# First batch of a Fourier mixing layer: own PSUM banks for the way back, another order inside each step, and two weight pieces finished later

## The chip, the cores and the metric

The kernel runs on one core of one Trainium2 chip. The metric is device time in microseconds (us) of one execution. TensorE does the matrix products, VectorE (DVE in the profile) and ScalarE (ACT) work on the results, GpSimd (POOL) does a few element-wise sums and issues transfers, SyncE (SP) issues most transfers.

## The reference

Two layers run one after the other. The first multiplies each of 8 batches, along its 3008 positions, by a filter in the frequency domain. The second is a two-layer network with an ELU between its two products. Cut to what matters:

```python
X = np.fft.rfft(x, axis=1)                       # x: (8, 3008, 256)
Y = X * (filt_r + 1j * filt_i)[None, :, :]       # filt: (1505, 256)
y = np.fft.irfft(Y, n=3008, axis=1).astype(np.float32)
h = y.reshape(24064, 256) @ w_in                 # w_in: (256, 2048)
g = np.where(h > 0, h, np.exp(np.minimum(h, 0)) - 1)
out = g @ w_out                                  # w_out: (2048, 256)
```

`w_in` and `w_out` arrive as 64-bit floats.

## The kernel before

**The transform.** 3008 is 47 x 64, so the transform is split into a short transform over 64 points, a multiplication by a table, and a transform over 47 points. For one batch the kernel has these stages. `a_unit` (`a_first` for batch 0) does the 64-point part for six groups of columns `c`. Then eight frequency groups `g` follow. `b_unit(b, g)` does the 47-point part on the way there and multiplies by the filter: eight records of TensorE matmuls into two PSUM banks, then four VectorE products (lines 309 to 312). `bi_unit(b, g)` is the 47-point part on the way back: sixteen records of matmuls into two banks, then two ScalarE copies out of them (lines 329 and 330). `y_write` sends the result to DRAM, and `y_read` and `n_unit` fetch it in another order and finish the transform for one of six column groups `m`.

**The first batch** goes without a trip through DRAM between its 64-point and its 47-point part. `t_first(g)` turns the stored result around by eight TensorE transposes into two PSUM banks `po`, which ScalarE copies out (line 270). Its way back takes both the filtered products and their second halves straight into the matmuls (`s[0]` and `s[1]` hold two tiles each), so nothing is added by GpSimd.

**The network.** The work on the 6 column groups of the 8 batches is cut into quads, one for each quarter `q` of the 2048 hidden columns. A quad has seven products up and seven products down (a Strassen-like scheme with seven products for eight), and ups of quad i are interleaved with downs of quad i-1. `plan` is an order written out by hand: `at(quad, place, fn)` puts a unit either in the middle of a quad (place 0) or at its end (place 1), and each engine runs its instructions in the order in which the program issues them.

**The weights** come in 16 pieces `k` of 512 columns x 128 rows, four to a quarter. `w_fetch(k)` brings a piece, `w_split(k)` (2 VectorE instructions) takes mantissa and exponent bits apart, `w_float(k)` (4 ScalarE instructions: two for the mantissa, two in `w_power` for the exponent) turns them into 32-bit floats, and `w_join(k)` (3 or 4 on VectorE) multiplies the two and stores the piece. After pieces 1, 3, 5, ... the join also runs `w_sums` (4 on VectorE), which forms the combinations that the seven products need; for piece 15 it is placed by itself. The pieces share two sets of work tiles `wtmp`, one for even and one for odd `k`; piece 15 uses the even one.

**PSUM.** There are eight banks: `po0` to `po3` (for `t_first`, later for the products down) and `m0` to `m3`, which `bank()` hands out in turn, the one freed first (in program order) being the first to be given again. From the third step of the first batch on, the same two of the four go to every `bi_unit` and the other two to every `b_unit`.

**The stretch that matters here** is the loop of the first batch at line 713, run for `g` from 0 to 9. In step `g` the program issues, in this order, the transposes for `g + 2`, the way back of `g - 2`, `w_float(g + 7)`, the forward unit of `g`, `y_write(0, g - 2)`, `w_join(g + 7)` and `w_split(g + 8)`, each where it applies. After it come the pieces 12 to 14, `y_read(0, 0)`, `n_unit(0, 0)` and then the quads.

Of the kernel before, what the change touches and what calls it, by code (L numbers as in the profile page):

```python
# [11 lines left out]
FP32 = mybir.dt.float32  # L12
# [14 lines left out]
P = 128  # L27
D = 256
# [6 lines left out]
NG = K2 // 4  # L35
# [78 lines left out]
def kernel(  # L114
# [25 lines left out]
    t2p = pool("t2p", 2)  # L140
# [3 lines left out]
    t4p = pool("t4p", 2)  # L144
# [4 lines left out]
    psO = pool("psO", 1, space=PSUM)  # L149
# [3 lines left out]
    gb, gr, gi = (gs[:, i] for i in range(3))  # L153
# [14 lines left out]
    banks = [0, 1, 2, 3]  # L168

    def bank(name, shape=(P, 2, D)):  # L170
        i = banks.pop(0)
        return i, psM.tile(list(shape), FP32, tag="m%d" % i, name=name)
# [86 lines left out]

    def t_first(g):  # L260

        t = t2s[0, g] = (t4p if g in (2, 3) else t2p).tile([P, 4, D], FP32, tag="t4" if g in (2, 3) else "t2", name="t2")
        for j in range(2):
            i = 2 * (g % 2) + j
            ps = psO.tile([P, 2, 256], FP32, name="po%d" % i)
            for u in range(2):
                k = 4 * g + 2 * j + u
                for dh in range(2):
                    nc.tensor.transpose(ps[0:ROWS, u, ts(dh, P)], zt[k // 16][dh][:, ts(k % 16, ROWS)], eye)
            nc.scalar.activation(out=t[0:ROWS, 2 * j:2 * j + 2, :], in_=ps[0:ROWS], func=AXT.Copy)  # L270
# [23 lines left out]
    def tile_mm(ps, table, k, rhs, special):  # L294
        for u, w, v in ((0, 1, 1), (1, 1, 0)) if special else ((0, 2, 0),):
            for n, r in enumerate(rhs):
                nc.tensor.matmul(ps[:, u:u + w, :], table[k, v, :], r[k, u:u + w, :], start=n == 0, stop=n == len(rhs) - 1)  # L297

    def b_unit(b, g, f=None, gb=gb, pq=None):
        t = t2s.pop((b, g))  # L300
        f = fbufs[(b * NG + g) % FBUFS] if f is None else f
        (i0, re), (i1, im) = (bank(n) for n in ("psr", "psi"))
        for o, a in ((0, 0), (64, 2)):
            for ps, k in ((re, LO), (im, HI)):
                tile_mm(ps[o:o + 64], gb, k, [t[:, a:a + 2, :]], g == 0 and a == 0)
        sr, si = (sp.tile([P, 2, D], FP32, tag=n, name=n) for n in ("sr", "si"))
        p, q = pq or (qp.tile([P, 2, D], FP32, tag=n, name=n) for n in ("sp", "sq"))

        nc.vector.tensor_tensor(out=sr, in0=re, in1=f[:, 0], op=ALU.mult)
        nc.vector.tensor_tensor(out=si, in0=re, in1=f[:, 1], op=ALU.mult)  # L310
        nc.vector.scalar_tensor_tensor(out=p, in0=im, scalar=-1.0, in1=f[:, 1], op0=ALU.mult, op1=ALU.mult)  # L311
        nc.vector.tensor_tensor(out=q, in0=im, in1=f[:, 0], op=ALU.mult)
        banks.extend((i0, i1))
        if b == 0:

            ss[b, g] = [sr, p], [si, q]
            return
        nc.gpsimd.tensor_tensor(out=sr, in0=sr, in1=p, op=ALU.add)  # L318
        nc.gpsimd.tensor_tensor(out=si, in0=si, in1=q, op=ALU.add)
        ss[b, g] = [sr], [si]  # L320

    def bi_unit(b, g):
        s = ss.pop((b, g))
        t = t3s[b, g] = t3p.tile([P, 4, D], FP32, tag="t3", name="t3")
        (i0, pa), (i1, pb) = (bank(n) for n in ("pva", "pvb"))
        for o, table, sv in ((0, gr, s[0]), (64, gi, s[1])):
            for ps, k in ((pa, LO), (pb, HI)):
                tile_mm(ps[o:o + 64], table, k, sv, g == 0 and k == LO)
        nc.scalar.activation(out=t[:, 0:2, :], in_=pa, func=AXT.Copy)  # L329
        nc.scalar.activation(out=t[:, 2:4, :], in_=pb, func=AXT.Copy)  # L330
        banks.extend((i0, i1))

    def y_write(b, g, queues=(nc.sync, nc.sync)):
        if g == 0:
# [236 lines left out]
    def w_split(k):  # L571
        m, e, c = wtmp[k % 2 if k < 15 else 0]
        f, l = c[:, 0], c[:, 1]
        wts[k] = m, e, f, l
        hi = wds[k][:, :, 1]
        nc.vector.tensor_scalar(out=m, in0=hi, scalar1=0x000FFFFF, scalar2=None, op0=ALU.bitwise_and)
        nc.vector.tensor_scalar(out=e, in0=hi, scalar1=0x7FF00000, scalar2=None, op0=ALU.bitwise_and)
# [66 lines left out]
    with tc.manual_schedule():  # L644


        with tc.tile_pool(name="boot", bufs=1) as bp:
            ff = bp.tile([P, NG, 2, 2, D], FP32, name="ff")
            once = bp.tile([P, 2, P], FP32, name="once")
            eye, gf = once[:, 0], once[:, 1].rearrange("p (v q) -> p v q", v=2)  # L650
            pq = [bp.tile([P, 2, D], FP32, name="pq%d" % i) for i in range(2)]
            zt[0] += [bp.tile([P, 16 * ROWS], FP32, name="zt%d" % i) for i in range(2)]

            for z in zt[0] + zt[1]:
                nc.gpsimd.memset(z.rearrange("p (k r) -> p k r", r=ROWS)[:, :, 48:64], 0.0)
            for k in (1, 2, 3):
                w_fetch(k)
            f_arrange()
            w_fetch(0, nc.sync)
            for c in range(NXC):  # L660
                x_place_first(c)
            for c in range(3):
                x_load_first(c)
            w_fetch(4, nc.sync)
            nc.scalar.memzero(ff[:, 0:NG // 2])
            nc.vector.memset(ff[:, NG // 2:NG], 0.0)
            wtmp.append([kp.tile([P, 512], U32, tag=t, name=n) for t, n in (("k0", "wm"), ("k1", "we"))] +
                        [kp.tile([P, 2, 512], FP32, tag="c", name="wfl")])
            wtmp.append([sdp.tile([P, 2, D], FP32, tag="sd", name=n).bitcast(U32).rearrange("p a b -> p (a b)")
                         for n in ("wm", "we")] +  # L670
                        [t1p.tile([P, XC, D], FP32, tag="t1", name="wfl").rearrange("p (a b) d -> p a (b d)", a=2)])
            for i, v in enumerate((1151.0 * 2 ** 23, 255.0 * 2 ** 23)):
                nc.vector.memset(edges[:, i:i + 1], v)

            def step(k):
                w_split(k)
                w_float(k)
                if k > 0:
                    w_join(k - 1)

            for k in range(3):
                step(k)
            w_fetch(5, nc.sync)
            for c in (3, 4):
                x_load_first(c)
            a_first(0)
            w_fetch(6, nc.sync)
            x_load_first(5)
            nc.sync.dma_start(once, once_d)
            nc.sync.dma_start(gs, gs_d)  # L690
            step(3)
            for c in (1, 2):
                a_first(c)
                w_fetch(c + 6, nc.sync)
            step(4)
            a_first(3)
            w_fetch(9, nc.sync)
            step(5)
            step(6)
            for c in (4, 5):  # L700
                a_first(c)
            tn_read(0, 0)
            for g in range(NG):
                f_read(0, g, ff[:, g])
                if 3 <= g < 5:
                    w_fetch(g + 7)
            for k in (12, 13, 14):
                w_fetch(k)
            w_split(7)
            w_join(6)  # L710
            for g in range(4):
                t_first(g)
            for g in range(NG + 2):
                if 2 <= g < NG - 2:
                    t_first(g + 2)
                if g >= 2:
                    bi_unit(0, g - 2)
                if g < 5:
                    w_float(g + 7)
                if g < NG:  # L720
                    b_unit(0, g, ff[:, g], gf, pq if g % 2 else None)
                if g >= 2:
                    y_write(0, g - 2, (nc.sync, nc.scalar if g == NG + 1 else nc.sync))
                if g < 4:
                    w_join(g + 7)
                    w_split(g + 8)
                if g == 7:
                    w_join(11)
                    w_split(12)
                    w_split(13)  # L730
            w_float(12)
            y_read(0, 0, (nc.sync, nc.scalar))
            w_float(13)
            w_join(12)
            w_fetch(15)
            w_split(14)
            w_join(13)
            w_float(14)
        for c in range(2):
            x_load(1, c)  # L740
        yp = pool("yp", 2)
# [1 line left out]
        ep = pool("ep", 2)  # L743
        op = pool("op", 1)
        n_unit(0, 0)
        w_join(14)

# [4 lines left out]
            plan.setdefault((quad, place), []).append((fn, a))  # L754


        for quad, place, fn, *a in ((0, 0, w_split, 15), (1, 1, w_float, 15, 0), (2, 0, w_float, 15, 1), (2, 1, w_join, 15),
                                    (3, 0, w_sums, 15)):
            at(quad, place, fn, *a)
        for c in range(2, XBUFS):  # L760
            at(c - 2, 0, x_load, 1, c)
# [85 lines left out]
```

## Time and profile before

| what | value |
|---|---|
| median of 4 runs | 2648.89 us (2647.28 to 2650.07) |
| the profiled execution's own time | 2647.28 us |
| its span, first to last instruction | 2645.5 us |
| PE busy | 2595.6 us (98% of the span) |
| DVE, ACT, POOL busy | 1844.0, 1507.7, 236.5 us |
| mean granted TensorE clock | 0.993 |
| PE, DVE, ACT busy from 0 to 100 us | 59.85, 70.26, 64.81 us |
| start of the loop's first forward unit on PE | 48.72 us |
| start of the last two copies of the way back (lines 329, 330) | 91.52 and 92.01 us |
| start of `n_unit(0, 0)` on PE | 100.03 us |
| first product of quad 0 | 103.57 us |

In a timeline row the first number is the start in us from the first instruction, the second the time it took, then engine, line, operation, output<-inputs, shapes and count. A square bracket tells how long the engine sat idle before the row and what ended that. Rows of like instructions that follow one another are merged (x16 is sixteen of them). In the table of windows each engine has its busy time and its number of instructions, and PEclk is the share of the TensorE clock that was granted.

### The profile page before, as it was taken

The page shows a single profiled execution, that of the slowest core. Times are in us where ns is not written, and L with a number is a line of the kernel's source. Part 1 is how long each engine was busy: PE and PEld are TensorE (multiplying, and loading weights), DVE is VectorE, ACT ScalarE, POOL GpSimd, SP SyncE. Part 2 cuts the span into 40 slices and gives each one's busy share as a digit, 9 for nine tenths or more (in the row PEclk, how much of TensorE's full clock was granted, in tenths as well). Part 3 has the DMA queues.
Part 4 walks back from the last instruction along what each step waited for, and adds up shares of the span by engine and source line. Part 5 has one row for each costly group of instructions (what it writes and reads, how often), then busy time and mean ns, then how long its engine had stood idle before and what let it go on. Part 6 is the DMA issues. An engine that isn't in the chain of part 4 may idle for free.

```text
span 2645.5 us, 37334 instructions
## 1 busy us (share of the span) xinstructions
PE 2595.6 (98%) x13508; PEld 2210.5 (84%) x13508; DVE 1844.0 (70%) x3203; ACT 1507.7 (57%) x2622; POOL 236.5 (9%) x298
## 2 busy tenths in 40 slices
PE   5899999999999999999999999999999999999998
PEld 4588789887898878988789888898789887898887
DVE  6777767677676776667767676666767677666666
ACT  6665555555556555655556555565555555555554
POOL 5001100012000210002100020001200011000000
PEclk8999999999999999999999999999999999999999
DMA  9534312523133331423214341134321333110010
GB/s 284 143 96 105 85 38 56 126 75 82 39 95 89 80 78 43 103 70 100 72 31 98 86 114 48 39 90 106 98 50 41 79 81 81 38 41 19 21 29 17
DMA packets 224456, 202.85 MB, mean 77 GB/s; under 512 B 127586, under 2 KB 191090, under 8 KB 224272
## 3 DMA queue, kind: packets, MB, share of 16 engines
q1 hardware_dynamic: 211632, 166.70, 25.2%
q0 software_dynamic: 11184, 33.04, 4.8%
q8 instruction: 107, 1.75, 0.3%
q10 hardware_dynamic: 1456, 0.72, 0.1%
q14 instruction: 77, 0.63, 0.1%
HBM read 128.52 MB, written 74.97 MB: 77 GB/s over the span
## 4 chain that ended last, share of the span: by engine, by line
PE 96%; DMA 2%; ACT 0%; DVE 0%; POOL 0%; issue 0%; ACTq 0%; DVEq 0%; SPq 0%; POOLq 0%
PE po L490 43%; PE phs L408 25%; PE phd L408 12%; PE pha L408 6%; PE psn L360 3%; PE pva L297 2%; PE psr L297 2%; PE psa L209 2%; DMA fd<-in_filt_i_dram 1%; DMA ff<-fd 0%; DMA wd<-in_moe_w_out_dram 0%; DMA fd<-in_filt_r_dram 0%; PE pvb L297 0%; DMA f<-in_moe_w_out_dram 0%; PE psi L297 0%
## 5 line engine op out<-in xcount | busy, mean ns | idle before, releaser
L490 PE MATMUL po<-g,wo 128*128 128x256 f32 (+1 forms) x5376 | 1296.7, 375 | 0.0
L490 PEld LDWEIGHTS po<-g,wo 128*128 128x128 f32 x5376 | 1015.0, 190 | 129.5 <-issue 15.8
L419 ACT ACTIVATE g<-phs 128x512 f32<-128x512 f32 (+1 forms) x576 | 338.7, 588 | 844.0 <-PE phs L408 843.4
L416 DVE TENSOR_TENSOR g<-phd,g 128x512 f32<-128x512 f32 (+1 forms) x384 | 259.6, 676 | 457.5 <-ACT e L426 282.5
L426 ACT ACTIVATE e<-e 128x512 f32<-128x512 f32 (+1 forms) x768 | 477.1, 621 | 24.3
L408 PE MATMUL phs<-y,wi 128*128 128x256 f32 (+1 forms) x1536 | 395.6, 380 | 0.0
L408 PE MATMUL phs<-ys,wi 128*128 128x256 f32 (+1 forms) x1536 | 387.6, 375 | 1.2 <-ACT g L419 1.2
L430 DVE SCALAR_TENSOR_TENSOR g<-e,g 128x512 f32<-128x512 f32 (+1 forms) x576 | 387.2, 672 | 0.0
L425 ACT ACTIVATE e<-g 128x512 f32<-128x512 f32 (+1 forms) x576 | 353.0, 613 | 32.2 <-DVE g L416 27.3
L408 PEld LDWEIGHTS phs<-y,wi 128*128 128x128 f32 x1536 | 285.1, 190 | 83.2 <-ACT t L329 34.1
L408 PEld LDWEIGHTS phs<-ys,wi 128*128 128x128 f32 x1536 | 291.5, 190 | 34.9 <-ACT g L419 1.9
L430 DVE SCALAR_TENSOR_TENSOR g<-e,phs 128x512 f32<-128x512 f32 (+1 forms) x192 | 129.9, 677 | 137.3 <-ACT e L426 137.1
L408 PE MATMUL phd<-ys,wi 128*128 128x256 f32 (+1 forms) x768 | 194.1, 375 | 0.2 <-DVE g L416 0.2
L408 PE MATMUL pha<-y,wi 128*128 128x256 f32 (+1 forms) x768 | 194.1, 375 | 0.0
L425 ACT ACTIVATE e<-phs 128x512 f32<-128x512 f32 (+1 forms) x192 | 112.9, 588 | 141.7 <-PE phs L408 140.8
L408 PE MATMUL phd<-y,wi 128*128 128x256 f32 (+1 forms) x768 | 193.7, 375 | 0.0
L318 POOL TENSOR_TENSOR sr<-sr,sp 128x512 f32<-128x512 f32 x56 | 71.2, 1271 | 1246.9 <-DVE sp L311 1246.9
L408 PEld LDWEIGHTS pha<-y,wi 128*128 128x128 f32 x768 | 146.4, 191 | 16.7
L408 PEld LDWEIGHTS phd<-ys,wi 128*128 128x128 f32 x768 | 145.5, 190 | 17.6 <-DVE g L416 1.3
L408 PEld LDWEIGHTS phd<-y,wi 128*128 128x128 f32 x768 | 145.8, 190 | 16.5
L467 DVE TENSOR_TENSOR g<-g,g 128x512 f32<-128x512 f32 (+1 forms) x192 | 130.7, 681 | 6.7
L470 DVE TENSOR_TENSOR g<-g,g 128x512 f32<-128x512 f32 (+1 forms) x192 | 130.7, 681 | 6.7
(133 smaller groups left out, 2366.6 us busy)
## 6 DMA issues: line engine op xcount, KB each, us to landing
yd<-t SPq DMA_DIRECT2D x127, 192.0 KB
t<-yd SPq DMA_DIRECT2D x190, 128.0 KB
z<-t SPq DMA_DIRECT2D x84, 256.0 KB
f<-fd POOLq DMA_DIRECT2D x112, 192.0 KB, 3.6
t<-z SPq DMA_DIRECT2D x224, 96.0 KB
out_dram<-o SPq DMA_DIRECT2D x632, 32.0 KB
tn<-tn_t SPq DMA_DIRECT2D x48, 256.0 KB
xc<-in_x_dram SPq DMA_DIRECT2D x84, 128.0 KB
```

Source lines behind the costliest of these rows:

```text
L297: nc.tensor.matmul(ps[:, u:u + w, :], table[k, v, :], r[k, u:u + w, :], start=n == 0, stop=n == len(rhs) - 1)
L318: nc.gpsimd.tensor_tensor(out=sr, in0=sr, in1=p, op=ALU.add)
L360: nc.tensor.matmul(ps[:, ts(q, P)], t[:, i - 4 * m, ds(dh * P, P)], w[:, i - 4 * m, :], start=True, stop=True)
L408: nc.tensor.matmul(ps[:, a, 0:h], w_in[q][:, COMBO[n], a, :], y[n], start=start and a == 0, stop=True, skip_group_check=True)
L416: nc.vector.tensor_tensor(out=g[o], in0=i0, in1=i1, op=ALU.add)
L419: nc.scalar.activation(out=g[o], in_=i0, func=AXT.Copy)
L425: nc.scalar.activation(out=e, in_=src, func=AXT.Relu, scale=-1.0)
L426: nc.scalar.activation(out=e, in_=e, func=AXT.Exp, scale=-1.0)
L430: nc.vector.scalar_tensor_tensor(out=g[n], in0=es[n], scalar=1.0, in1=src, op0=ALU.subtract, op1=ALU.max)
L467: nc.vector.tensor_tensor(out=b12, in0=b22, in1=b12, op=ALU.subtract)
L470: nc.vector.tensor_tensor(out=g["t4"], in0=g["b21"], in1=g["t2"], op=ALU.subtract)
L490: nc.tensor.matmul(po[i][:, u, 0:h], w_out[q][:, COMBO[n], a, :], g[n][:, a, :], start=q == 0 and a == 0 and n in (1, 3, 6, 4), stop=True, ...
```

## The change

- `bi_unit` of batch 0 takes the banks `po2` and `po3` instead of two from `bank()`; `t_first` uses `po0` and `po1` alone. The four banks of `bank()` are left to the forward units.
- In each step the matmuls of the forward unit come first, then the whole way back of `g - 2` (a function handed to `b_unit` as `between`), then the four VectorE products of the forward unit.
- The transposes for `g + 4` follow in the same step, four steps ahead instead of two; groups 6 and 7 take tiles of the pool `t4p` as groups 2 and 3 do.
- `w_float(g + 7)` stands behind the transposes. `w_join(10)` moves from step 3 to step 7, `w_split(11)` from step 3 to step 2.
- Piece 14: half of its `w_float` moves to the end of quad 0, its join to the middle of quad 1. Piece 15: the split moves from the middle of quad 0 to the end of quad 1, the halves of `w_float` from the end of quad 1 and the middle of quad 2 to the middle and end of quad 2, the join from the end of quad 2 to the middle of quad 3, the sums from the middle to the end of quad 3.
- At the start, `w_fetch(4)` is issued ahead of `x_load_first(2)`.

```diff
     def t_first(g):
-        t = t2s[0, g] = (t4p if g in (2, 3) else t2p).tile([P, 4, D], FP32, tag="t4" if g in (2, 3) else "t2", name="t2")
+        pool, tag = (t4p, "t4") if g % 4 > 1 else (t2p, "t2")
+        t = t2s[0, g] = pool.tile([P, 4, D], FP32, tag=tag, name="t2")
         for j in range(2):
-            i = 2 * (g % 2) + j
-            ps = psO.tile([P, 2, 256], FP32, name="po%d" % i)
+            ps = psO.tile([P, 2, 256], FP32, tag="po%d" % j, name="po%d" % j)
...
-    def b_unit(b, g, f=None, gb=gb, pq=None):
+    def b_unit(b, g, f=None, gb=gb, pq=None, between=None):
...
                 tile_mm(ps[o:o + 64], gb, k, [t[:, a:a + 2, :]], g == 0 and a == 0)
+        if between:
+            between()
...
     def bi_unit(b, g):
...
-        (i0, pa), (i1, pb) = (bank(n) for n in ("pva", "pvb"))
+        if b == 0:
+            pa, pb = (psO.tile([P, 2, 256], FP32, tag="po%d" % i, name="po%d" % i) for i in (2, 3))
+        else:
+            (i0, pa), (i1, pb) = (bank(n) for n in ("pva", "pvb"))
...
-        banks.extend((i0, i1))
+        if b > 0:
+            banks.extend((i0, i1))
...
-            for c in range(3):
+            for c in range(2):
                 x_load_first(c)
             w_fetch(4, nc.sync)
+            x_load_first(2)
...
             for g in range(NG + 2):
-                if 2 <= g < NG - 2:
-                    t_first(g + 2)
-                if g >= 2:
-                    bi_unit(0, g - 2)
+                back = (lambda g=g: bi_unit(0, g - 2)) if g >= 2 else None
+                if g < NG:
+                    b_unit(0, g, ff[:, g], gf, pq if g % 2 else None, back)
+                else:
+                    back()
+                if g < 4:
+                    t_first(g + 4)
                 if g < 5:
                     w_float(g + 7)
-                if g < NG:
-                    b_unit(0, g, ff[:, g], gf, pq if g % 2 else None)
+                if g < 3:
+                    w_join(g + 7)
+                    w_split(g + 8)
+                if g == 2:
+                    w_split(11)
                 if g >= 2:
                     y_write(0, g - 2, (nc.sync, nc.scalar if g == NG + 1 else nc.sync))
-                if g < 4:
-                    w_join(g + 7)
-                    w_split(g + 8)
                 if g == 7:
+                    w_join(10)
                     w_join(11)
                     w_split(12)
                     w_split(13)
...
             w_split(14)
+            w_float(14, 0)
             w_join(13)
-            w_float(14)
...
         n_unit(0, 0)
-        w_join(14)
...
-        for quad, place, fn, *a in ((0, 0, w_split, 15), (1, 1, w_float, 15, 0), (2, 0, w_float, 15, 1), (2, 1, w_join, 15),
-                                    (3, 0, w_sums, 15)):
+        for quad, place, fn, *a in ((0, 1, w_float, 14, 1), (1, 0, w_join, 14), (1, 1, w_split, 15), (2, 0, w_float, 15, 0),
+                                    (2, 1, w_float, 15, 1), (3, 0, w_join, 15), (3, 1, w_sums, 15)):
             at(quad, place, fn, *a)
```

## The prediction

> **What bounds the kernel now.** The page says first that TensorE (PE) is busy for 2595.6 of 2645.5 us. From the first quads on it hardly waits: what is not PE lies in the first 116 us, and only there can this change act. I read that stretch by windows.
>
> ```profile
> 51.40:58.20 6.80, 4.40 (x27) 2.12 (x25) 6.66 (x15) 2.20 (x5) 4.75 (x9) 1.00 1.01 256
> 58.20:65.00 6.80, 5.95 (x24) 2.53 (x28) 6.76 (x13) 6.20 (x12) 2.84 (x5) 0.50 1.03 215
> 65.00:74.70 9.70, 8.37 (x64) 3.28 (x56) 9.53 (x21) 5.58 (x11) 0.00 (x0) 1.00 0.56 199
> 74.70:92.60 17.90, 14.98 (x104) 5.74 (x104) 12.73 (x23) 9.27 (x17) 0.00 (x0) 1.00 0.45 111
> ```
>
> After the stretch's length come the busy times of PE, its weight loads, VectorE, ScalarE and POOL. VectorE's: 6.66 of 6.80, 6.76 of 6.80, 9.53 of 9.70. Up to 74.7 us VectorE is the bound; then it has 5 us free of 17.9 and something else binds. The last three numbers of a row are the granted clock, the DMA share and GB/s: the clock is at half from 58.2 to 65.0. VectorE's timeline tells where its free time lies:
>
> ```profile
> 53.20 0.68 DVE L599 SCALAR_TENSOR_TENSOR we<-wd,we 128x512 uint32<-128x512 uint32 x1
> ...
> 78.13 0.69 DVE L309 TENSOR_TENSOR sr<-psr,ff 128x512 f32<-128x512 f32 x1 [1.26 <-PE psi L297]
> ...
> 86.86 0.69 DVE L309 TENSOR_TENSOR sr<-psr,ff 128x512 f32<-128x512 f32 x1 [1.26 <-PE psi L297]
> ```
>
> Forward units 5, 6 and 7 wait for their matmuls by 1.26, 2.51 and 1.26 us, as their two banks are read out before they are filled again. ScalarE and PE show the other loop and two places in the quads:
>
> ```profile
> 49.60 0.74 ACT L584 ACTIVATE wfl<-wd 128x512 f32<-128x512 uint32 x1
> ...
> 79.14 0.60 ACT L329 ACTIVATE t<-pva 128x512 f32<-128x512 f32 x1
> ...
> 82.27 0.60 ACT L329 ACTIVATE t<-pva 128x512 f32<-128x512 f32 x1 [2.05 <-PE pvb L297]
> ...
> 91.52 0.60 ACT L329 ACTIVATE t<-pva 128x512 f32<-128x512 f32 x1 [1.79 <-PE pvb L297]
> ...
> 114.02 0.53 ACT L419 ACTIVATE g<-phs 128x448 f32<-128x448 f32 x1
> ```
>
> ```profile
> 82.92 1.07 PE L297 MATMUL pva<-sr,gs 48*64 48x512 f32 x2
> ...
> 114.59 1.02 PE L408 MATMUL phs<-ys,wi 128*128 128x224 f32 x4 [0.60 <-ACT g L419]
> ...
> 153.01 1.68 PE L490 MATMUL po<-g,wo 128*128 128x224 f32 x8
> ```
>
> The way back of group 4 is copied out from 82.27, and that of group 5 starts at 82.92, as the first copy ends: one pair of banks, 2.0 us of matmuls and two copies of 0.5 and 0.6 in turn, 3.1 us a group. From group 3 (copied from 79.14) to group 7 (91.52) that is 12.4 us for four. Its end sets the rest: written to DRAM, read back, `n_unit` at 100.03.
>
> **Own banks.** The forward units get two pairs, so the idle 1.26, 2.51 and 1.26 us can go. The way back still has one pair, so its 3.1 us a group stay, now with the forward matmuls (0.9 us, the row group from 66.28) in the gap of the copies. What counts is when group 3 starts it.
>
> **VectorE up to that point.** In the change the transposes of the first four groups have two banks instead of four. Before, eight copies run from 45.77 at 0.5 us each. With two banks a copy (0.6), four transposes (0.6 from start to end) and two signals follow one another in 1.3 us a pair: the last transposes end at about 50.1 instead of 48.8, the forward matmuls of group 0 at 51.2, and its products at 53.7 (before: 53.2). `w_float(7)`, at 49.60 before, now stands behind the copies of the transposes for group 4, which stand behind forward unit 0 on PE. These copies end at 52.7 and the float takes 2.5 more: 55.25. `w_join(7)` is queued on VectorE for that, with everything behind it: 1.55 us of new idle, 2.05 us later than the row at 53.20.
> From there to the end of the products of group 3, in us by the rows: join 7 3.7, split 0.7, products 2.4, join 8 1.9, split 0.7, products 2.4, join 9 3.6, splits 10 and 11 1.4, products 2.4, together 19.2: 74.45. Before it is 71.72. Group 4 then ends at 76.85, against 76.78 before: `w_join(10)` (2.0 us, rows from 71.72) no longer stands there, but the two delays and split 11 have eaten it.
>
> **The way back.** Forward matmuls of group 5 need the bank that the products of group 3 free at 74.45; they end at 75.4 and the way back of group 3 at 77.5. Its copies start 1.6 us ahead of 79.14, and at 3.1 us a group those of group 7 at 89.9. Group 5's products now wait for that way back too (it comes first in their bank of `sr`), but the way back is the slower of the two, and this costs nothing more: products of group 7 end at 86.2, one unit after the way back of group 5.
> What is late next: behind them VectorE has join 10 and join 11 (2.0 and 3.7), then split 12, which gives `w_float(12)` its mantissa at 92.3 and ScalarE the end of it at 94.25; before it ends at 95.5. Half of `y_read(0, 0)` stands behind it on ScalarE's queue. So of 1.6 us 1.25 reach `n_unit`.
>
> **The clock.** PE now idles from about 71.5 to 74.5, as its work is done early. Before, after 2.76 us of idle (56.29 to 59.05) the clock was at half from 58.20 for 6.8 us. The same here would make the forward unit (0.95 us) and the way back of group 3 (1.65 us) slower: between nothing and 2.6 us. The row is close to the case, and the phase of the drop is open; I take the middle, 1.3. The gain of the first batch is then 1.25 - 1.3, about nothing; its ends are a gain of 1.25 and a loss of 1.35.
> The Trainium skill says on its page "TensorE: Matmul & The Clock Gate", Part 1, that the clock falls after at least one idle window of about 3.4 us and comes back after a busy one. By that rule a pause of 3.0 us would leave the clock alone and the sum would be 1.3 us lower; the trace's drop after 1.9 us of idle disagrees, and I go by the trace.
>
> **The quads.** Quad 0 has no products down, and ScalarE binds it: copies, Relu and Exp follow one another without a pause from 112.93 to the copy at 114.02, for which PE waits 0.60 us. The half of `w_float(14)` that before ran at 99.87 to 101.3, while ScalarE waited, now stands right before that copy: two instructions, 1.3 us by the rows from 94.17 to 95.50. All of it goes on PE. That `w_join(14)` and split 15 leave VectorE there (2.0 and 0.7 us) brings nothing, as ScalarE, not VectorE, is late. Bounds: 0 (if Exp ends earlier) and 1.3; I take 1.3.
> `w_join(14)` in quad 1 (2.1 us) fits into 2.51 us that VectorE idles ahead of 120.73: nothing. `w_float(15)` at an end of a quad already stood at such a place and stopped nobody: nothing.
> `w_join(15)` in quad 3 is 0.45 us longer than the sums that stood there, ahead of the addition at 146.54 with no idle time: 0.2 us on PE.
> `w_sums(15)` moves behind quad 3's last VectorE work, which ends at 152.6. The third of the four sums, which product 3 needs, ends 1.35 later (rows from 55.31), at 153.95; PE wants it at 153.01. That is 1.0 us; bounds 0.5 and 1.3. Nothing behind absorbs it: in the page's groups the phs products wait 1.2 us for ScalarE in the whole run, and both waits lie in quads 0 and 1.
> Together 2.5 us, from 1.5 to 2.8.
>
> **The start.** Piece 4 (512 KB) ahead of group 2 of x on SP: from its ninth transfer on, SP issues one when the eighth before it has landed (the one at 10.08 after a landing at 10.06, that at 12.86 after 12.78). The same bytes stand ahead of group 5 of x, the last to arrive and PE's release at 40.90. Group 2's matmuls at 23.81 come some 1.5 us later; ScalarE's 2.03 us of idle ahead of 38.31 takes that up: nothing, at most 1.5. POOL's queue keeps its order.
>
> **Sum.** 2.5 + 0.05 = 2.6 us more. The profiled execution took 2647.28, 1.78 more than its span; the median stands 1.61 above it. I add to the median: 2651.5. With the ends of the two parts, from 1.5 - 1.25 to 2.8 + 1.35: 2649.1 to 2653.0. A measurement of this kernel tells about 0.2% from no change, 5.3 us: this is no change.
>
> **Rivals.** *The clock stays low (slower).* If the half clock holds on beyond group 3, each further way back is 1.7 us longer (four rounds of 0.43 us at 0.85). With no gain lost twice, the sum is 2.5 - 1.25 + 0.95 + 1.7 for each slow group: it passes 5.3 us from the second on; two or three give 2654.5 to 2656.2. For it: 6.8 us of half clock before is about two such groups with their forward units. Against: PE was at the full clock through the whole of 74.7 to 92.6, with gaps. I put it at 2655.4.
> *The way back keeps pace with VectorE (faster).* If no wait for `w_float(7)` arises and the copies hide, group 7's products end at 72.9 + 4 x 2.4 = 82.5, and `w_float(12)` at 90.5 instead of 95.5: 5.0 us, and if the quads hide their pieces, 2643.9. Against: the 3.1 us a group, which the one pair of banks sets, and ScalarE's order.
> *The start moves (part of the change does nothing).* Piece 4 does not come earlier to any use, and group 2's delay reaches the transposes: 1.5 us more, 2653.0.
>
> **Chances.** Forecast 0.55, start 0.10, low clock 0.22, pace 0.13. Faster takes 0.08 of the pace case, which straddles 2643.6; slower all of the low clock and 0.05 of the others' upper ends; the rest is the same. The range leaves out the pace case and the topmost of the low clock: 2647.0 to 2656.5.
>
> **What would show it.** Right: `w_join(7)` idle before it with ScalarE's L593 as releaser, way back of group 7 copied out at 89.9 to 92.5, `n_unit` at 98.8 to 101.4, an idle of 1.8 us before PE's third product of quad 1, one of 1.0 before product 3 of the fifth quad. Wrong: the copies of the way back less than 3.0 us apart, PE without a pause at quad 1 or 5, or any change after 170 us.

## The result, and the profile after

The changed kernel takes 2650.9 us (median of 41 runs, 2646.45 to 2656.91) against 2647.31 of the kernel before in the same session (61 runs, 2643.25 to 2650.44). The ratio is 1.0014, with a 95% interval of 1.001 to 1.0019: 3.6 us more, from 2.6 to 5.0 by the interval. Foretold were 2.6 us more. The profiled execution of after took 2651.09 us for a span of 2649.3, at a granted clock of 0.992.

Lines of the code below the diff's first places have moved: the products of the forward unit are L311 to L314 (before L309 to L312), the copies of the way back L334 and L335, the float step L590 to L599, the join's first operation L605 (before L599), the products of the quads L414 and L496, `n_unit`'s matmuls L366 and the four sums L626 to L629.

The windows of after, in the same columns as before (length, busy time of PE, weight loads, VectorE, ScalarE, POOL, then granted clock, DMA share, GB/s):

```profile
60.10:66.90 6.80, 6.80 (x28) 2.26 (x27) 6.77 (x12) 5.04 (x10) 2.09 (x4) 0.50 1.03 294
66.90:73.70 6.80, 5.07 (x40) 1.86 (x40) 6.66 (x16) 5.84 (x12) 0.00 (x0) 1.00 0.44 146
73.80:77.10 3.30, 3.30 (x24) 1.06 (x18) 2.38 (x4) 1.31 (x2) 0.00 (x0) 0.50 0.41 105
77.20:91.60 14.40, 11.64 (x84) 3.84 (x77) 12.29 (x23) 5.42 (x10) 0.00 (x0) 1.00 0.43 110
114.70:118.10 3.40, 3.40 (x9) 3.11 (x10) 3.37 (x7) 0.55 (x1) 0.00 (x0) 0.50 0.01 3
```

Besides the stretch at half clock that before has, there are two more: 3.3 us where the way back of group 3 runs (third row), and 3.4 us in quad 1 (last row). From 60.1 to 73.7 VectorE is still full; of the 14.4 us from 77.2 on it has 2.1 free. Its timeline (start, us, engine, line, operation; in brackets the idle time before it and what ended it):

```profile
53.79 0.69 DVE L605 SCALAR_TENSOR_TENSOR we<-wd,we 128x512 uint32<-128x512 uint32 x1 [1.69 <-ACT we L599]
...
76.42 0.69 DVE L311 TENSOR_TENSOR sr<-psr,ff 128x512 f32<-128x512 f32 x1 [0.92 <-PE po L297]
...
83.51 0.69 DVE L311 TENSOR_TENSOR sr<-psr,ff 128x512 f32<-128x512 f32 x1 [0.65 <-PE po L297]
```

The waits ahead of the products of units 5 to 7 are shorter (0.92 and 0.65 here, where before had 1.26, 2.51 and 1.26), and something else ends them: the matmuls of the way back (`po`), which read the tile that the product is to overwrite, where before it was the unit's own matmuls (`psi`). The new wait ahead of `w_join(7)` is there: 1.69 us, ended by the float step on ScalarE. ScalarE's timeline shows that float step, the way back's first copies, and the half of `w_float(14)` that now stands ahead of a copy of quad 0:

```profile
51.20 0.68 ACT L590 ACTIVATE wfl<-wd 128x512 f32<-128x512 uint32 x1
...
77.72 0.60 ACT L334 ACTIVATE t<-po 128x512 f32<-128x512 f32 x1 [2.57 <-PE po L297]
...
80.86 0.60 ACT L334 ACTIVATE t<-po 128x512 f32<-128x512 f32 x1 [2.05 <-PE po L297]
...
90.46 0.60 ACT L334 ACTIVATE t<-po 128x512 f32<-128x512 f32 x1 [2.13 <-PE po L297]
...
112.73 0.71 ACT L598 ACTIVATE we<-we,edges 128x512 f32<-128x512 uint32 x1
113.46 0.72 ACT L599 ACTIVATE we<-we,edges 128x512 uint32<-128x512 f32 x1
114.09 0.52 ACT L425 ACTIVATE g<-phs 128x448 f32<-128x448 f32 x1
```

The way back of groups 3 to 7 is copied at 77.72, 80.86 and so on to 90.46: 12.7 us for four, 3.2 a group. On PE the three waits of the quads stand:

```profile
98.95 3.75 PE L366 MATMUL psn<-tn,t 128*128 128x128 f32 x16 [8.60 <-DMA t<-yd]
...
114.67 1.85 PE L414 MATMUL phs<-ys,wi 128*128 128x224 f32 x4 [2.26 <-ACT g L425]
116.31 2.58 PE L496 MATMUL po<-g,wo 128*128 128x224 f32 x8
...
142.24 1.02 PE L414 MATMUL phs<-ys,wi 128*128 128x224 f32 x4 [0.20 <-ACT g L425]
...
156.18 1.78 PE L496 MATMUL po<-g,wo 128*128 128x224 f32 x8 [0.78 <-DVE wo L628]
```

2.26 us for the copy behind the float step, 0.20 for the next such copy, 0.78 for the third sum. The four matmuls behind the first wait take 1.85 us where four took 1.02 before: they run at half clock.

In this execution `n_unit` starts 1.1 us sooner than before (98.95 against 100.03), and from the first product of quad 0 to the last matmul PE needs 2537.6 us against 2533.6, 4.0 more. But the first transposes had also started 1.7 us sooner (42.73 against 44.45). So three questions went to the chip: whether the start was moved by its edit, which part the loss belongs to, and how much of these differences one execution has by chance.

### The profile page after: what moved, and what is told of

It reads as the page before. It is cut to its first block, busy times and chain, and to the rows that moved or that the text cites. A ratio compares the mean times of both kernels' runs of the same rounds, so it can differ in the third digit from the quotient of the medians.

```text
span 2649.3 us, 37321 instructions
## 1 busy us (share of the span) xinstructions
PE 2599.2 (98%) x13508; PEld 2211.5 (83%) x13508; DVE 1844.2 (70%) x3203; ACT 1507.9 (57%) x2622; POOL 236.3 (9%) x298
## 4 chain that ended last, share of the span: by engine, by line
PE 96%; ACT 1%; DVE 0%; DMA 0%; issue 0%; DVEq 0%; SPq 0%
PE po L496 43%; PE phs L414 25%; PE phd L414 12%; PE pha L414 6%; PE psn L366 3%; PE pva L297 2%; PE psr L297 2%; PE psa L209 2%; PE po L297 0%; PE psi L297 0%; PE pvb L297 0%; DMA t<-yd 0%; ACT e L431 0%; DMA yd<-t 0%; ACT e L432 0%
## 5 line engine op out<-in xcount | busy, mean ns | idle before, releaser
L496 PE MATMUL po<-g,wo 128*128 128x256 f32 (+1 forms) x5376 | 1297.7, 376 | 0.8 <-DVE wo L628 0.8
L496 PEld LDWEIGHTS po<-g,wo 128*128 128x128 f32 x5376 | 1015.8, 190 | 130.9 <-issue 15.8
L414 PE MATMUL phs<-y,wi 128*128 128x256 f32 (+1 forms) x1536 | 395.6, 380 | 0.0
L414 PE MATMUL phs<-ys,wi 128*128 128x256 f32 (+1 forms) x1536 | 388.5, 375 | 3.1 <-ACT g L425 3.1
L414 PEld LDWEIGHTS phs<-y,wi 128*128 128x128 f32 x1536 | 285.1, 190 | 83.2 <-ACT t L334 34.1
L414 PEld LDWEIGHTS phs<-ys,wi 128*128 128x128 f32 x1536 | 291.9, 190 | 37.2 <-ACT g L425 4.1
L414 PE MATMUL pha<-y,wi 128*128 128x256 f32 (+1 forms) x768 | 193.9, 375 | 0.0
L414 PE MATMUL phd<-ys,wi 128*128 128x256 f32 (+1 forms) x768 | 193.8, 375 | 0.0
L414 PE MATMUL phd<-y,wi 128*128 128x256 f32 (+1 forms) x768 | 193.7, 375 | 0.0
L414 PEld LDWEIGHTS pha<-y,wi 128*128 128x128 f32 x768 | 146.2, 190 | 16.6
L414 PEld LDWEIGHTS phd<-ys,wi 128*128 128x128 f32 x768 | 145.7, 190 | 16.7 <-DVE g L422 0.2
L414 PEld LDWEIGHTS phd<-y,wi 128*128 128x128 f32 x768 | 145.8, 190 | 16.5
```

Source lines behind the costliest of these rows:

```text
L414: nc.tensor.matmul(ps[:, a, 0:h], w_in[q][:, COMBO[n], a, :], y[n], start=start and a == 0, stop=True, skip_group_check=True)
L496: nc.tensor.matmul(po[i][:, u, 0:h], w_out[q][:, COMBO[n], a, :], g[n][:, a, :], start=q == 0 and a == 0 and n in (1, 3, 6, 4), stop=True, ...
```

## The experiments

The theory at first: the start edit brought the transposes 1.7 us forward, and the quads lose more than that by their three waits. Rivals: the 1.7 us are chance; the new loop loses the time; the clock does.

**The spread of one kernel.** Both kernels were profiled once more, unchanged.

> Before, unchanged, for one more profile. If the start is chance, its last 64-point unit starts anywhere from 39.4 to 42.3 us (40.90 in the first profile); if it is set by the order, within 0.3 of 40.90. From its first transposes to n_unit: 55.6 us in the first profile; 58 to 60.5 if half a clock falls into the last way backs.

> The changed kernel, unchanged, for one more profile. Wait of 2.26 us ahead of the third product of quad 1, 0.2 in quad 3, 0.78 in the fifth quad, again; last 64-point unit anywhere from 39.4 to 42.3 us; from the first transposes to n_unit 54 to 57 us, according to the clock at the way back of group 3.

Measured, in one execution each: 2649.93 us for before and 2647.86 for after, the other way round than the medians. In this execution before has its last way backs at half clock, as its first profile had not; after has them at full clock. The windows, of before again:

```profile
82.70:86.10 3.40, 3.40 (x20) 1.53 (x14) 0.00 (x0) 1.08 (x2) 0.00 (x0) 0.50 0.44 112
```

and after again:

```profile
70.80:91.00 20.20, 16.98 (x124) 5.66 (x119) 18.65 (x36) 10.77 (x19) 0.00 (x0) 1.00 0.39 99
```

A drop on the last way backs thus belongs to the execution and not to one of the kernels. The table puts all profiles side by side: start of the first transposes, time from there to `n_unit`, time from the first product of quad 0 to the last matmul, and where the first batch ran at half clock past 70 us.

| kernel | transposes | to `n_unit` | quads on | half clock |
|---|---|---|---|---|
| before | 44.45 | 55.58 | 2533.6 | none |
| before again | 45.30 | 58.08 | 2533.1 | 82.7–86.1 |
| before, new start | 45.11 | 58.20 | 2533.1 | to 70.4, 80.6–87.4 |
| before, new quads | 42.73 | 60.41 | 2535.6 | 80.4–87.3 |
| after | 42.73 | 56.22 | 2537.6 | 73.8–77.2 |
| after again | 43.67 | 54.73 | 2535.2 | to 70.8 |
| after, old start | 42.30 | 57.04 | 2537.8 | 71.1–77.9 |
| after, whole `w_float(14)` early | 43.59 | 56.37 | 2534.6 | 74.8–78.2 |
| after, sums sooner | 45.77 | 56.45 | 2534.1 | 77.9–81.3 |
| after, old quads | 45.38 | 54.35 | 2532.7 | to 72.5 |
| after, old quads, + `w_float(7)` first | 42.87 | 54.94 | 2533.0 | 72.2–75.6 |
| + two pairs | 43.14 | 53.54 | 2532.8 | 70.0–76.8 |
| + split 12 early | 43.85 | 53.73 | 2533.0 | 72.3–79.1 |
| + last way back in a free tile | 43.88 | 52.65 | 2532.9 | 70.8–77.6 |

**The start.** Its order back in after, and its new order alone in before:

```
-            for c in range(2):
+            for c in range(3):
                 x_load_first(c)
             w_fetch(4, nc.sync)
-            x_load_first(2)
```

> The changed kernel with its order at the start as before: group 2 of x is fetched ahead of piece 4 again. Theory: the changed order is what brings the last 64-point unit of the first batch from 40.90 to 39.39 us and n_unit to 98.95; then that unit starts at 40.9 here, n_unit at 100.4, and the time is 1.5 us over the changed kernel (1.4 + 3.6 over before, 5.0 us). Rival: the 1.5 us are chance of one execution; then the unit starts anywhere from 39 to 41 and the time equals the changed kernel's (3.6 us over before).

> Before with the start's new order alone. Theory (the order brings it): last 64-point unit at 39.4 instead of 40.9, n_unit at 98.6, 1.5 us under before. Rival (chance): the time of before within 0.7 us.

After with the old start takes 2651.65 us, 1.0014 times before (1.0005 to 1.0023), the same ratio as with the new one; the new start alone takes 2647.36, 0.9996 (0.9987 to 1.0005). In the table both orders start early in some executions and late in others (42.30 with the old order, 45.77 with the new). The 1.7 us are chance; that part of the theory has fallen.

**The quads.** Pieces 14 and 15 placed as before, in after; and their new placing alone, in before. The first edit is shown; the second is the same one turned round:

```
-            w_float(14, 0)
             w_join(13)
+            w_float(14)
...
         n_unit(0, 0)
+        w_join(14)
...
-        ... ((0, 1, w_float, 14, 1), (1, 0, w_join, 14), (1, 1, w_split, 15), (2, 0, w_float, 15, 0),
-             (2, 1, w_float, 15, 1), (3, 0, w_join, 15), (3, 1, w_sums, 15)):
+        ... ((0, 0, w_split, 15), (1, 1, w_float, 15, 0), (2, 0, w_float, 15, 1), (2, 1, w_join, 15),
+             (3, 0, w_sums, 15)):
```

> The changed kernel with pieces 14 and 15 placed as before. Theory: the quads' new places cost the changed kernel 4.2 us (1.15 us of wait in quad 1, 1.6 of half clock behind it, 0.2 in quad 3, 0.8 to 1.0 in the fifth quad); without them n_unit stays at 98.95, the wait in quad 1 is 0.6 us, the fifth quad has none, and the time is 4.2 us under the changed kernel, 0.6 under before. Rival: piece 14 done ahead of quad 0 delays n_unit or its combinations in the changed order; then n_unit or the first product is at least 1 us later than 98.95 and 102.50, and less than 3 us come back.

> Before with the new places of pieces 14 and 15 alone. Theory: 4.2 us over before, with about 2.3 us of wait ahead of the third product of quad 1 and about 0.8 ahead of the second product down of the fifth quad. Rival: the waits depend on the loop's new order; then under 2 us over before.

With the old quads after takes 2646.78 us, 0.9999 times before (0.999 to 1.0007): no loss is left. The new quads alone take 2650.55, 1.0012 (1.0003 to 1.002): 3.2 us of loss without the new loop, where 4.2 were expected. PE's timeline of the latter has the three waits of after almost to the digit:

```profile
118.55 1.02 PE L408 MATMUL phs<-ys,wi 128*128 128x224 f32 x4 [2.27 <-ACT g L419]
...
144.45 1.02 PE L408 MATMUL phs<-ys,wi 128*128 128x224 f32 x4 [0.21 <-ACT g L419]
...
158.39 1.78 PE L490 MATMUL po<-g,wo 128*128 128x224 f32 x8 [0.78 <-DVE wo L622]
```

So the loss is the quads', whatever loop runs before. Here the four matmuls behind the 2.27 us take 1.02: no half clock. The table's column "quads on" prices both cases. Old quads: 2533.0 us in the mean of eight. New quads without a drop behind the wait (after again, and before with the new quads): 2535.2 and 2535.6, 2.2 to 2.6 more. With a drop (after, and after with the old start): 2537.6 and 2537.8, 4.6 to 4.8 more.

The traces also tell which executions get the drop. In each of them the granted clock changes only on a grid of 3.41 us of its own; in the first profile of after, for instance, at 73.75, 77.17, 94.23, 104.47, 114.71 and 118.13. Rows by this grid around the pause, first of after, then two in a row of before with the new quads (windows):

```profile
111.30:114.71 3.41, 1.15 (x7) 0.80 (x5) 3.34 (x7) 3.11 (x6) 0.00 (x0) 1.00 0.85 177
```

```profile
114.58:117.99 3.41, 1.71 (x10) 1.36 (x8) 3.38 (x7) 3.17 (x7) 0.00 (x0) 1.00 1.06 219
117.99:121.40 3.41, 2.85 (x15) 2.85 (x16) 3.34 (x7) 1.05 (x3) 0.00 (x0) 1.00 0.36 81
```

In after, and in after with the old start, the pause lies wholly in one stretch of the grid, PE is busy for 1.15 us of it, and the next stretch runs at half clock. In the other three executions with the same pause a border of the grid cuts it in two, PE is busy for at least 1.71 us of either stretch, and the clock stays up. So the place of the pause on the grid decides here. How short a pause may be is not settled by this: elsewhere between 36 and 125 us, stretches with 1.3 to 1.7 us of idle time were followed by half clock in some cases and not in others.

**The two waits apart.** In after, the whole of `w_float(14)` ahead of quad 0; and the sums of piece 15 in the middle of quad 3 instead of at its end:

```
-            w_float(14, 0)
+            w_float(14)
...
-        ... ((0, 1, w_float, 14, 1), (1, 0, w_join, 14), ...
+        ... ((1, 0, w_join, 14), ...
```

> The changed kernel with the second half of w_float(14) back ahead of quad 0; its join stays in quad 1, piece 15 stays as changed. Theory: those two ScalarE instructions in front of quad 1's copy are the whole wait of 2.26 us there; here it is 0.6 to 1.2 us, the waits of 0.2 and 0.78 us in quads 3 and 4 stay, and the time falls 1.3 to 3 us under the changed kernel (0.6 to 2.3 over before). Rival: w_join(14) in the middle of quad 1 or the late pieces bind there too; then the wait stays over 1.8 us.

```
-        ... (3, 1, w_sums, 15)):
+        ... (3, 0, w_sums, 15)):
```

> The changed kernel with w_sums(15) in the middle of quad 3, behind its join, instead of at its end. Theory: the wait of 0.78 us ahead of the second product down of the fifth quad is the sums' place alone and goes; those of 2.26 and 0.2 stay; 0.7 to 1.0 us under the changed kernel (2.6 to 2.9 over before). Rival: join and sums together (3.7 us) hold the addition of product 7 in quad 3, and a wait of 0.5 us or more comes there instead.

The first takes 2648.76 us, 1.0003 (0.9994 to 1.0013). Its third product of quad 1 waits less (0.90 instead of 2.26 us), and the sums' wait stays (PE's timeline):

```profile
114.32 1.02 PE L414 MATMUL phs<-ys,wi 128*128 128x224 f32 x4 [0.90 <-ACT g L425]
...
154.16 1.78 PE L496 MATMUL po<-g,wo 128*128 128x224 f32 x8 [0.78 <-DVE wo L628]
```

The second takes 2648.57, 1.0008 (0.9999 to 1.0017); in it the waits on ScalarE stay and that on the sums is gone:

```profile
116.88 1.02 PE L414 MATMUL phs<-ys,wi 128*128 128x224 f32 x4 [2.27 <-ACT g L425]
...
142.77 1.02 PE L414 MATMUL phs<-ys,wi 128*128 128x224 f32 x4 [0.20 <-ACT g L425]
```

Each wait goes with the piece named for it. The times agree in sign; their intervals meet that of after (1.001 to 1.0019), so the sizes are better read from "quads on": 2534.6 and 2534.1, against 2535.2 to 2537.8.

**What the new loop was held up by.** On after with the old quads, three edits, each on top of the one before, and then a fourth. First, `w_float(7)` ahead of the loop, so that nothing stands between it and `w_join(7)`:

```
+            w_float(7)
...
-                if g < 5:
+                if 0 < g < 5:
                     w_float(g + 7)
```

> The changed kernel with the quads as before, and w_float(7) ahead of the loop, so ScalarE does it before the copies for group 4. Theory: VectorE's 1.69 us of idle ahead of w_join(7) goes, the products of group 3 end 1.6 us sooner after the first transposes, and n_unit starts 52.7 us after them (54.35 in the changed kernel with the quads as before); time 1.0 to 1.6 us under that kernel. Rival: the copies for group 4 come late instead, group 4's forward unit waits, and n_unit does not move by 0.5 us.

2644.82 us, 0.9993 (0.9984 to 1.0002). The idle ahead of `w_join(7)` is gone, but `n_unit` comes 54.94 us after the first transposes (54.35 without the edit; 52.7 expected). PE idles 3.33 us ahead of the forward matmuls of group 5, and the clock is at half from 72.2 to 75.6. The time is some 2 us under that of before, with an interval that includes no change.

Then two pairs of banks in turn for the way back of the groups from 3 on, as the transposes no longer need theirs:

```
-            ... for i in (2, 3))
+            ... for i in ((0, 1) if g > 2 and g % 2 else (2, 3)))
```

> As the kernel with w_float(7) first, and the way back of groups 3, 5 and 7 in po0 and po1, so it has two pairs of banks. Theory: the copies of the way back then come 2.6 us apart or less instead of 3.1 to 3.2 (VectorE's 2.4 or PE's 2.6 sets it), the last ends about 2 us sooner, but ScalarE's w_float(12), behind joins 10 and 11 on VectorE, holds half of y_read: n_unit starts 51 to 52 us after the first transposes. Rival: PE's own work sets 3.1 us; then the copies stay 3.1 apart and nothing moves.

2643.18 us, 0.9987 (0.9979 to 0.9996): 3.4 us under before, with an interval that leaves out no change. ScalarE's timeline:

```profile
77.67 0.60 ACT L334 ACTIVATE t<-po 128x512 f32<-128x512 f32 x1 [2.83 <-PE po L297]
...
80.27 0.60 ACT L334 ACTIVATE t<-po 128x512 f32<-128x512 f32 x1 [1.51 <-PE po L297]
...
82.89 0.60 ACT L334 ACTIVATE t<-po 128x512 f32<-128x512 f32 x1 [1.54 <-PE po L297]
...
84.61 0.60 ACT L334 ACTIVATE t<-po 128x512 f32<-128x512 f32 x1 [0.63 <-PE po L297]
...
88.19 0.60 ACT L334 ACTIVATE t<-po 128x512 f32<-128x512 f32 x1 [2.49 <-DMA yd<-t]
```

2.6, 2.6 and 1.7 us a group instead of 3.1 to 3.2: the pair of banks was what set the pace. The last copy waits 2.49 us for something new: its tile of the way back is still being written to DRAM. Split 12 ahead of join 11, so that `w_float(12)` comes sooner on ScalarE, adds nothing to this:

```
                     w_join(10)
+                    w_split(12)
                     w_join(11)
-                    w_split(12)
                     w_split(13)
```

> As the kernel with two pairs, and split 12 ahead of join 11 on VectorE, so that w_float(12) can go 3.7 us sooner. Theory: y_read then waits for the last y_write alone; n_unit starts 50 us after the first transposes, 4 us sooner than with the changed loop, and the time is 4 us under before. Rival: the later joins 12 and 13 on VectorE then hold the combinations of n_unit, and the first product that needs them waits over 1.5 us; under 2.5 us gained.

2643.1 us, 0.9987 (0.9978 to 0.9995), 53.73 to `n_unit` where 50 was expected. `w_float(12)` was not what came last any more; the last copy still waits 2.52 us for its tile. So the fourth edit gives that copy a tile which the transposes no longer use:

```
-        t = t3s[b, g] = t3p.tile([P, 4, D], FP32, tag="t3", name="t3")
+        t = t3s[b, g] = (t2p.tile([P, 4, D], FP32, tag="t2", name="t3") if (b, g) == (0, 7) else
+                         t3p.tile([P, 4, D], FP32, tag="t3", name="t3"))
```

> As the kernel with two pairs and split 12 early, and the way back of group 7 put into a free tile of another pool, so that it needs no tile whose write to DRAM is still on its way. Theory: the 2.5 us that the last copies waited for a write go, they start 42 to 43 us after the first transposes (45.4 before this edit) and n_unit 51.5 us after them; time 1.5 to 2.5 us under the kernel with two pairs, 5 to 6 under before. Rival: y_read then waits for w_float(12) or for the write all the same, and n_unit moves by less than 0.7 us.

2643.33 us, 0.9984 (0.9976 to 0.9993). The copy comes 1.67 us behind the one before it (84.81), with no wait for DRAM (ScalarE's timeline), but the transfer is late next: on SP's queue the read back waits for the writes (waits on SP's queue: us in total, times, longest):

```profile
86.48 0.60 ACT L335 ACTIVATE t<-po 128x512 f32<-128x512 f32 x1 [0.58 <-PE po L297]
```

```profile
SPq L354 <- DMA yd<-t: 4.0, 1, 4.0
```

The last writes, issued at 87.62, land at 92.0; the reads go out at 92.05 and 92.19. `n_unit` comes 52.65 us after the transposes (51.5 expected), the shortest of all, but the time of this version can't be told from the two before it, where 1.5 to 2.5 us less were expected. The best ratio seen is thus 0.9984 to 0.9987, 3.4 to 4.2 us under before.

## Why the prediction was right, and where its terms were off

It put the loss in the quads at 2.5 us, the first batch at nothing, and the sum at 2.6. Measured are 3.6 (2.6 to 5.0), and the time with the old quads is that of before. Step by step:

- **`w_float(7)` and `w_join(7)`**: 1.55 us of idle foretold, released by ScalarE; 1.69 measured, by ScalarE. The products of group 3 end at 73.03 instead of 74.45, 1.4 sooner; the start had been 1.7 us early by chance.
- **The way back's pace**: 3.1 us a group foretold, 3.1 to 3.2 measured, and with a second pair of banks 1.7 to 2.6. The shorter waits on VectorE, now for the way back's reading of the tile, were off the path, as foretold.
- **The clock at group 3**: the drop came, for 3.4 us (73.75 to 77.2), and the copies of group 3 at 77.72 where 77.5 had been put, without the drop and from a start 1.7 us later. The size was right for that execution, the pause was not: 3.0 us of idle time on PE were foretold, and it idled 1.61 us, ending at 71.97, because the second of group 3's four products already frees the first of its two banks. So the size came out right for another pause than the one reckoned with. What I missed is that before meets such a drop too, in three of its loop's four profiles, later and up to 6.8 us long.
- **The first batch**: 0.05 us of loss foretold, a gain of 1.25 less 1.3 for the clock. Both parts show when one counts from the loop's first product on VectorE to `n_unit`: 49.2 us in the profile of before without a late drop (50.80 to 100.03), 47.5 and 47.9 with the new loop where the clock is up from 72.5 or 70.8 on, and 49.3 to 49.5 in the three with a drop of 3.4 us (49.1 in the one with 6.8). Whether a gain is left in the mean is another matter. From the transposes on, the profiles alone would give one: the old loop needs 58.07 us to `n_unit` in the mean of four, the new 55.86 in that of six. But those four executions lay 1.8 us above the medians of their kernels in the mean, and the six 0.2 below; if all of that lies in the first batch, it takes 2.0 of the 2.2 away. The times agree: 0.9999 with the old quads. Whether the new loop gains a microsecond stays open.
- **Quad 0 and the half of `w_float(14)`**: 1.3 us foretold. The wait grew from 0.60 to 2.26 us, by more than 1.3 (1.8 had been named as the sign). But another wait went away, for VectorE ahead of a product of quad 0: 0.19 us in before, 1.16 in after with the old quads. That taking `w_join(14)` out of VectorE's way "brings nothing" was thus wrong. The two waits together are 0.72 to 1.16 us in the eight profiles with the old quads, so 2.26 is 1.1 to 1.5 more. The term of 1.3 holds.
- **The clock behind that wait**: this term is missing in the prediction. In two of the five executions with the new float place (after, after with the old start) the pause of 2.3 us is followed by 3.4 us at half clock, as it lies in one stretch of the clock's grid. They lie 2.0 to 2.6 us above the others with all three waits ("quads on"). Two in five of that is 0.9 us, about what the sum lacks: 2.5 + 0.9 = 3.4, where the new quads cost 3.2 us alone and 4.0 in the new loop (1.0014 less 0.9999). That two in five is also the share in all runs is not shown; the wider spread of after (10.5 us against 7.2) fits it.
- **`w_float(15)` and `w_join(15)`**: foretold 0 and 0.2; measured 0.20 on PE in quad 3, but released by ScalarE's copy behind the second half of `w_float(15)`, at the end of quad 2. The size fits by luck: the step that it "already stood at such a place and stopped nobody" failed, and the join stopped nobody: VectorE idles 1.87 us ahead of the addition that it was to delay.
- **`w_sums(15)`**: 1.0 us foretold, 0.78 measured, gone when the sums move.
- **The start**: nothing foretold, nothing measured in either kernel.
- **The rivals**: a clock that stays low beyond group 3 did not come in the two profiles of after; the drop in quad 1 cost about 2 us, not 5. That the way back keeps pace came only with a second pair of banks and `w_float(7)` sooner, and gave, with the quads as before, 3.4 to 4.2 of the 5.0 us. The start does nothing to the time, for better or worse.
- **The rule weighed against the trace**: in quad 1 the clock fell behind a pause of 2.26 us in two executions and stayed up behind the same pause (2.27) in three, and at group 3 it fell behind one of 1.61. The Trainium skill's page "TensorE: Matmul & The Clock Gate", Part 1, has the clock fall after at least one idle window of about 3.4 us; the trace disagrees, since PE need not be idle for all of a stretch. The drops lasted 3.4, 6.8, 10.2 or (before with the new quads, 53.1 to 66.8) 13.7 us, whole numbers of such stretches. That the clock comes back after a busy window, as the same page has it, agrees with the drops of 3.4 us, in which PE was busy throughout (3.40 of 3.40); but in before with the new quads a drop lasted 6.8 us with PE busy for all 6.80. Going by the trace was right.

## What to carry over

A step that costs nothing on an engine with idle time can cost its whole length when it is put right ahead of the copy that the bound engine waits for: ask what is queued behind it, not how busy the engine is. When a pause of the bound engine is added, price the clock drop that may follow it, in its own sentence and with a chance. And when the difference sought is of the size by which one execution differs from the next, profile both kernels twice before reading a gain or a loss out of two traces.

## What was not expected of the hardware

- The same loop has its half clock at other places in other executions. From its first product on VectorE to `n_unit` the old loop takes 49.2 us with no late drop, 51.0 with one of 3.4 us and 52.1 and 52.5 with one of 6.8 us: about half of the drop's length. The rest of the range from 55.58 to 60.41 us in the table lies ahead of that product; in before with the new quads, with the earliest transposes of the four, the product waits for the filter's transfer (5.49 us idle, ended by a DMA). In the run of before with the new quads, the drop lay on the last way backs (windows):

```profile
80.40:87.20 6.80, 6.80 (x33) 2.57 (x35) 1.70 (x4) 1.13 (x3) 0.00 (x0) 0.50 0.36 88
```

- PE was waiting for nobody in that stretch: a row of matmuls at half clock was the bound, with VectorE and ScalarE nearly idle beside it (1.70 and 1.13 of 6.80 us).
- The first transposes start anywhere from 42.30 to 45.30 us with the old order of the start's loads, and from 42.73 to 45.77 with the new.
